# Contiguous transposes for the first two supertiles, and stores that put their rows right

## The chip, the cores and the metric

The kernel runs on one core of a Trainium2 chip. The metric is the device time of one execution in microseconds (us), as the median of several runs. The profile is one execution; its span, from the first to the last instruction, is some 2 us shorter than the device time.

## The reference

A depthwise convolution with a 1x1 window is a scale per channel, and a pointwise convolution is a matrix product over the channels:

```python
# x: (1, 384, 384, 384) bf16, dw: (1, 1, 384), pw: (384, 384)
out = x * dw[0, 0]                            # k = 1, so no padding and one term
return jnp.einsum('bhwc,cd->bhwd', out, pw)
```

So 147456 rows of 384 channels are each multiplied by the same 384x384 matrix, whose rows were scaled by dw. The kernel scales the matrix once, at its start, and not the rows.

## The kernel before

Rows are worked on in *supertiles* of 512, of which there are 288. Supertiles are loaded and stored in *chunks* of L supertiles; chunks make up *groups*, and a group uses one of three input buffers X and one of three output buffers O. The first group has the chunks 1, 1, 2, 2, 4; each group in the middle is one chunk of 10; the last two groups have shrinking chunks.

```python
LMAX, NR = 10, 3
head, tail = [[1, 1, 2, 2, 4]], [[6, 4], [4, 2, 1, 1]]
return head + [[LMAX]] * (mid // LMAX) + tail
# chunks: (g, i, off, first, L): group, place in it, offset in the buffer, first supertile, length
n_parts = [1 if c[0] + 1 < len(groups) else len(PARTS) if c[3] + 1 == NS else 2 for c in chunks]
```

TensorE multiplies over partitions, so the channels must lie on partitions. VectorE does this with transposes of 32x32 blocks of 4-byte words (two channels in a word), two for each supertile (`h` = 0, 1), into one of two buffers T. PSUM has one half of four banks for each of two supertiles. The main loop keeps TensorE on 48 matmuls per supertile, four row tiles side by side:

```python
def supertile(s, rv):
    for b, par in steps:                       # 12 steps
        for q in range(4):                     # PSUM bank q takes the rows from row tile q
            if q == 0 and par == 0 and b in (0, 3):
                nc.tensor.wait_ge(s_t[s][b // 3], rv)          # transposes h = 0, h = 1
            if q == 0 and s == 0:
                for e, v in w_first.get((b, par), []):         # weight casts, early steps
                    nc.tensor.wait_ge(s_wr[e], v)
            mm = nc.tensor.matmul(PS[s][:, q, :D], lhsT=Ts[s][32 * q : 32 * q + 32, b, par::2],
                                  rhs=w_r[32 * q : 32 * q + 32, b, par, :], ...)

# of the scaled matrix, six casts from PSUM: 1 ScalarE, 0 VectorE
w_eng = [1, 0, 1, 1, 1, 1]
# the first step of supertile 0 waits for one cast of VectorE and three of ScalarE
w_first = {(0, 0): [(0, 1), (1, 3)], (4, 0): [(1, 4)], (4, 1): [(1, 5)]}
```

The transposes, in which `k` counts the four rows per partition of a supertile and `i` the 32 partitions of a block:

```python
def transposes(t, j):
    ...
    X, sem, n = x_of(t)
    Xw = X.bitcast(U32).rearrange("p (k l) c -> p k l c", l=L)
    Tw = Ts[s][:].bitcast(U32).rearrange("p b (i k) -> p b k i", k=4)
    for h in range(2):
        if h == 0 and j == 0:
            nc.vector.wait_ge(sem, n)                          # the chunk has landed
        ins = nc.vector.transpose(
            out=Tw[:, 3 * h : 3 * h + 3],
            in_=Xw[:, :, j, 96 * h : 96 * h + 96].rearrange("p k (b w) -> p b k w", w=32),
        )
        if jj >= 2:
            ins._wait_ge(s_pe, 2 * (jj - 2) + h + 1)           # T is free again
        ins.then_inc(s_t[s][h])
```

The innermost run of the output, over `i`, steps 4 words (16 bytes), so that a row's place in T is its place in the supertile. The last supertile has a form of its own (`T<-Xk` in the profile), whose output is one run.

ScalarE copies the four banks of a finished supertile from PSUM to the output buffer O, as bf16:

```python
if j == 0 and i == 0 and g >= NR:                              # the buffer's last stores are out
    nc.scalar.wait_ge(s_o[g % NR], 16 * sum(map(len, groups[g % NR : g : NR])))
a = nc.scalar.copy(Ov[:, :, j, :], PS[s][:, :, :D])            # (p, q, d)
a._wait_ge(s_pe, 2 * jj + 2)
a.then_inc(s_a[s])
```

All loads of the main loop and nearly all stores are issued by SyncE, one after the other, in a fixed order. A group's load waits until the buffer's last supertile has been transposed, and a store until the copy of its last supertile is done:

```python
def store(t, k):
    g, i, off, first, L = chunks[t]
    je = first + L * (k + 1) // n_parts[t] - 1
    src = Os[g % NR][:, 4 * off * D : 4 * (off + L) * D]
    rows = of[512 * first : 512 * (first + L), :]
    if first + 2 < NS:
        dst = rows.rearrange("(q p j) d -> p q (j d)", q=4, p=P)
        src = src.rearrange("p (q e) -> p q e", q=4)
        e = L * D // n_parts[t]
        dst, src = dst[:, :, e * k : e * k + e], src[:, :, e * k : e * k + e]
        nc.sync.wait_ge(s_a[je % 2], je // 2 + 2)
    ...                                                        # the last two supertiles
    eng = nc.scalar if first + 1 == NS and k == 2 else nc.sync
    eng.dma_start(dst, src).then_inc(s_o[g % NR], 16)

for _, f, a in sorted(todo, key=lambda a: a[0]):
    if f is load_x and chunks[a[0]][4] == LMAX and chunks[a[0]][0] == 1:
        nc.sync.wait_ge(x_of(1)[1], 16)
    if f is store and a[0] == 0:
        for _ in range(28):                                    # waits that are over at once: a short delay
            nc.sync.wait_ge(s_pw, 16)
    f(*a)
```

SyncE's order at the start is: the loads of the first group's five chunks, the loads of the second and third group, the stores of chunks 0 to 3, the load of the fourth group, the store of chunk 4, and from there a load and a store of a group in turn.

Of the kernel before, what the change touches and what calls it, by code (L numbers as in the profile page):

```python
# [9 lines left out]
U32 = mybir.dt.uint32  # L10
# [3 lines left out]
NR = 3  # L14
LONG_AT = [8, 148]
PARTS = [slice(0, 4, 2), slice(1, 2), slice(3, 4)]


def _groups(n_super: int):

    head, tail = [[1, 1, 2, 2, 4]], [[6, 4], [4, 2, 1, 1]]
    mid = n_super - sum(map(sum, head + tail))
    assert mid > 0 and mid % LMAX == 0
    return head + [[LMAX]] * (mid // LMAX) + tail
# [3 lines left out]
def kernel(  # L28
# [12 lines left out]
    nc = tc.nc  # L41
# [3 lines left out]
    D = pw.shape[1]  # L45
# [7 lines left out]
    NS = N // 512  # L53
    groups = _groups(NS)

    chunks, first = [], 0
# [2 lines left out]
            chunks.append((g, i, sum(ls[:i]), first, L))  # L59
            first += L  # L60
    NT = len(chunks)
    n_parts = [1 if c[0] + 1 < len(groups) else len(PARTS) if c[3] + 1 == NS else 2 for c in chunks]
    g_end = [max(c[3] + c[4] for c in chunks if c[0] == g) - 1 for g in range(len(groups))]

    consts = ctx.enter_context(tc.tile_pool(name="consts", bufs=1))
# [19 lines left out]
    Ts = [bufp.tile([P, NB, 256], BF16, name=f"T{i}") for i in range(2)]  # L85
# [9 lines left out]
    s_a = [nc.alloc_semaphore(f"s_a{i}") for i in range(2)]  # L95
    s_d = nc.alloc_semaphore("s_d")
    s_o = [nc.alloc_semaphore(f"s_o{i}") for i in range(NR)]
# [10 lines left out]
    with tc.tile_critical(sync_engine=mybir.EngineType.Pool, no_gpsimd_drain=True):  # L108
        def x_of(t):
            g, i, off, first, L = chunks[t]  # L110
            if first + 2 == NS:
                return Xl[:], s_xl, 32
            n = sum(len(ls) > i for ls in groups[g % NR : g + 1 : NR])
            return Xs[g % NR][:, 4 * off : 4 * (off + L), :], s_x[g % NR][i], 16 * n

        def load_x(t, eng=nc.sync):
            g, i, off, first, L = chunks[t]
            dst, sem, _ = x_of(t)
            rows = xf[512 * first : 512 * (first + L), :]
            if first + 2 < NS:  # L120
                src = rows.rearrange("(p s) c -> p (s c)", p=P)
                dst = dst.rearrange("p s c -> p (s c)")
                if i == 0 and g >= NR:
                    je = g_end[g - NR]
                    eng.wait_ge(s_t[je % 2][1], je // 2 + 1)
            else:
                src = rows.rearrange("(a k q) c -> q a k c", k=4, q=4)
            eng.dma_start(dst, src).then_inc(sem, 16)

        def load_last(eng):  # L130
            src = xf[512 * (NS - 1) :, :].rearrange("(m p) c -> p m c", p=P)
            eng.dma_start(Xl[:], src).then_inc(s_xl, 16)

        def store(t, k):
            g, i, off, first, L = chunks[t]
            je = first + L * (k + 1) // n_parts[t] - 1
            src = Os[g % NR][:, 4 * off * D : 4 * (off + L) * D]
            rows = of[512 * first : 512 * (first + L), :]
            if first + 2 < NS:
                dst = rows.rearrange("(q p j) d -> p q (j d)", q=4, p=P)  # L140
                src = src.rearrange("p (q e) -> p q e", q=4)
                e = L * D // n_parts[t]
                dst, src = dst[:, :, e * k : e * k + e], src[:, :, e * k : e * k + e]
                nc.sync.wait_ge(s_a[je % 2], je // 2 + 2)
            elif first + 2 == NS:
                dst = rows.rearrange("(m q) d -> m (q d)", q=4)
                part = slice(2 * D * k, 2 * D * k + 2 * D)
                dst, src = dst[:, part], src[:, part]
                nc.sync.wait_ge(*((s_a[0], NS // 2 + 1) if k == 0 else (s_d, 1)))
            else:  # L150
                dst = rows.rearrange("(m p) d -> p m d", p=P)[:, PARTS[k], :]
                src = src.rearrange("p (m d) -> p m d", d=D)[:, PARTS[k], :]
                if k == 0:
                    nc.sync.wait_ge(s_d, 2)
                    nc.sync.wait_ge(s_a[1], NS // 2 + 1)
                elif k == 1:
                    nc.sync.wait_ge(s_d, 3)
                else:
                    nc.scalar.wait_ge(s_a[1], NS // 2 + 2)
            eng = nc.scalar if first + 1 == NS and k == 2 else nc.sync  # L160
            eng.dma_start(dst, src).then_inc(s_o[g % NR], 16)
# [10 lines left out]
        for t, (g, i, off, first, L) in enumerate(chunks):  # L172
            if 0 < t < NT - 2:
                todo.append((g_end[g - NR] if g >= NR else -1, load_x, (t,)))
            for k in range(n_parts[t] - (first + 1 == NS)):
                todo.append((first + L * (k + 1) // n_parts[t] + 1, store, (t, k)))
        for _, f, a in sorted(todo, key=lambda a: a[0]):
            if f is load_x and chunks[a[0]][4] == LMAX and chunks[a[0]][0] == 1:
                nc.sync.wait_ge(x_of(1)[1], 16)
            if f is store and a[0] == 0:  # L180

                for _ in range(28):
                    nc.sync.wait_ge(s_pw, 16)
            f(*a)
# [128 lines left out]
        for n in range(4):  # L313
            rows = slice(32 * n, 32 * n + 32)
# [3 lines left out]
        for n in range(4):  # L318
            to, h, e = slice(32 * n, 32 * n + 32), n // 2, n % 2
            for g in range(4):  # L320
                rows = slice(32 * g, 32 * g + 32)
# [8 lines left out]
        def transposes(t, j):  # L330
            g, i, off, first, L = chunks[t]
            jj = first + j
            s = jj % 2
            if jj + 1 == NS:
                nc.vector.wait_ge(s_xk, 32)
                Tw = Ts[s][:].bitcast(U32).rearrange("p (v j) (m w) -> p v j m w", v=2, m=4)
                Xw = Xk[:].bitcast(U32).rearrange("p (j v m) w -> p v j m w", v=2, m=4)
                for v in range(2):
                    ins = nc.vector.transpose(out=Tw[:, v], in_=Xw[:, v])  # L339
                    ins._wait_ge(s_pe, 2 * (jj - 2) + v + 1)  # L340
                    ins.then_inc(s_t[s][v])
                return
            X, sem, n = x_of(t)
            Xw = X.bitcast(U32).rearrange("p (k l) c -> p k l c", l=L)
            Tw = Ts[s][:].bitcast(U32).rearrange("p b (i k) -> p b k i", k=4)
            for h in range(2):
                if h == 0 and j == 0:
                    nc.vector.wait_ge(sem, n)
# [4 lines that stand above are left out]
                if jj >= 2:  # L353
                    ins._wait_ge(s_pe, 2 * (jj - 2) + h + 1)
                ins.then_inc(s_t[s][h])

        order = [(t, j) for t in range(NT) for j in range(chunks[t][4])]

# [26 lines left out]
        for jj, (t, j) in enumerate(order):  # L385
            g, i, off, first, L = chunks[t]
            s = jj % 2
            Ov = Os[g % NR][:, 4 * off * D : 4 * (off + L) * D].rearrange("p (q j d) -> p q j d", q=4, d=D)
            if j == 0 and i == 0 and g >= NR:
                nc.scalar.wait_ge(s_o[g % NR], 16 * sum(map(len, groups[g % NR : g : NR])))  # L390
            if jj + 2 == NS:
                nc.vector.wait_ge(s_pe, 2 * jj + 2)
                nc.vector.wait_ge(s_o[g % NR], 16 * sum(map(len, groups[g % NR : g : NR])))
                a = nc.scalar.copy(Ov[:, 0:2, j, :], PS[s][:, 0:2, :D])  # L394
                a._wait_ge(s_pe, 2 * jj + 2)
                a.then_inc(s_a[s])
                nc.vector.tensor_copy(Ov[:, 2:4, j, :], PS[s][:, 2:4, :D]).then_inc(s_d)  # L397
                continue
            if jj + 1 == NS:
                for n, m in enumerate((0, 2, 1, 3)):  # L400
                    o = (nc.scalar.copy if n % 2 else nc.vector.tensor_copy)(Ov[:, m, j, :], PS[s][:, m, :D])  # L401
                    o._wait_ge(s_pe, 2 * jj + 1 + n)
                    o.then_inc(s_a[s] if n % 2 else s_d)
                store(t, 2)
                continue
            a = nc.scalar.copy(Ov[:, :, j, :], PS[s][:, :, :D])  # L406
            a._wait_ge(s_pe, 2 * jj + 2)
            a.then_inc(s_a[s])

            if jj == LONG_AT[0]:  # L410
                load_last(nc.scalar)
            if jj == LONG_AT[1]:
                nc.scalar.wait_ge(s_xk, 32)
                load_x(NT - 2, nc.scalar)
            if jj + 2 < NS:
                transposes(*order[jj + 2])
# [30 lines left out]
```

## Time and profile before

| | |
|---|---|
| device time, median of 3 runs | 574.56 us (574.37 to 574.73) |
| span of the profile | 572.3 us |
| TensorE matmul busy | 567.0 us, 99% |
| VectorE busy | 508.9 us, 89% |
| ScalarE busy | 418.2 us, 73% |
| granted TensorE clock | 1.00 |
| DMA | 226.88 MB, 396 GB/s over the span |

The busy times are sums over the whole span. The chain that ended last follows the work back from the last instruction, at each step to what released it. A group's row gives the busy time, the mean time of one instruction in ns, the idle time of the engine just before the group's instructions, and what ended this idle time. For a DMA, the issue (the time in which SyncE handed it to the queue) and the landing (when its semaphore reached its full count) are different things, and the landing can be much later.

### The profile page before, as it was taken

What the parts mean: (1) busy time and instruction counts of PE and PEld (TensorE: products, weight loads), DVE (VectorE), ACT (ScalarE), POOL (GpSimd) and SP (SyncE); (2) the same over time, 40 slices, a digit from 0 to 9 for tenths busy, and PEclk for the clock granted to TensorE, in tenths of its full rate; (3) what the DMA queues carried; (4) which work ended last, traced back from release to release, by engine and by line L of the source; (5) the groups of instructions that cost most, each with busy time, mean ns of one, the idle gap of its engine ahead of it and who ended that gap; (6) DMA issues with size and microseconds to landing.
All of it is one profiled execution on the core that took longest, in us unless ns stands there. A gap on an engine that the chain in (4) does not pass through costs nothing.

```text
span 572.3 us, 29681 instructions
## 1 busy us (share of the span) xinstructions
PE 567.0 (99%) x13835; PEld 414.0 (72%) x13835; DVE 508.9 (89%) x585; ACT 418.2 (73%) x297; POOL 16.9 (3%) x45
## 2 busy tenths in 40 slices
PE   8999999999999999999999999999999999999997
PEld 5777777777777777777777777777777777777774
DVE  7899999999999999999999999999999999999995
ACT  6777777777777777777777777777777777777775
POOL 4042000000000000000000000000000000000000
PEclk9999999999999999999999999999999999999999
DMA  8999999999999999999999999999999999999677
GB/s 328 446 387 424 420 420 424 437 420 419 424 420 412 395 386 434 399 388 400 414 406 396 410 419 392 403 403 432 398 384 422 417 382 390 420 403 386 252 287 256
DMA packets 26896, 226.88 MB, mean 396 GB/s; under 512 B 1285, under 2 KB 7558, under 8 KB 23046
## 3 DMA queue, kind: packets, MB, share of 16 engines
q1 hardware_dynamic: 25696, 225.91, 97.4%
q10 hardware_dynamic: 1190, 0.89, 0.5%
q14 instruction: 9, 0.07, 0.0%
q8 instruction: 1, 0.02, 0.0%
HBM read 113.54 MB, written 113.25 MB: 396 GB/s over the span
## 4 chain that ended last, share of the span: by engine, by line
PE 98%; DMA 1%; DVE 0%; SPq 0%; issue 0%; ACT 0%; POOLq 0%
PE ps L211 98%; DMA X<-in_x_dram 1%; PE ps L279 0%; DVE T L349 0%; ACT O L401 0%; SPq L168 0%; SPq L167 0%; SPq L442 0%; POOLq L108 0%; POOLq L431 0%
## 5 line engine op out<-in xcount | busy, mean ns | idle before, releaser
L211 PE MATMUL ps<-w_r,T 32*128 32x384 bf16 x13776 | 559.8, 321 | 0.4 <-DVE T L349 0.4
L349 DVE STREAM_TRANSPOSE T<-X 128x384 uint32<-128x384 uint32 x572 | 501.6, 880 | 54.5 <-DMA X<-in_x_dram 2.0
L211 PEld LDWEIGHTS ps<-w_r,T 32*128 32x128 bf16 x13776 | 411.6, 93 | 148.7 <-issue 0.8
L406 ACT CAST O<-ps 128x1536 bf16<-128x1536 f32 x286 | 411.3, 1438 | 147.0 <-PE ps L211 147.0
L326 POOL COPY Xk<-Xl 32x256 bf16<-32x256 bf16 (+1 forms) x32 | 10.1, 340 | 22.5 <-DMA Xl<-in_x_dram 21.6
L316 POOL COPY raw<-w_r 32x768 bf16<-32x768 bf16 x8 | 6.4, 819 | 6.6 <-ACT w_r L362 6.4
L362 ACT CAST w_r<-ps 128x768 bf16<-128x768 f32 x5 | 3.6, 820 | 1.0 <-PE ps L261 1.0
L228 PE MATMUL ps<-const-bfloat16-1.0 32*128 32x384 bf16 x24 | 2.4, 513 | 1.1 <-PEq L431 1.1
L261 PE MATMUL ps<-raw 64*128 64x384 bf16 x16 | 2.6, 475 | 0.1
L261 PEld LDWEIGHTS ps<-raw 64*128 64x128 bf16 x16 | 0.8, 114 | 2.2 <-DMA raw<-in_pw_dram 1.2
L328 ACT ACT_TABLE_LOAD x1 | 1.3, 1283 | 1.5 <-PEq L431 1.5
L279 PE MATMUL ps<-raw,T 64*128 64x384 bf16 (+1 forms) x16 | 2.2, 326 | 0.0
L397 DVE CAST O<-ps 128x768 bf16<-128x768 f32 x1 | 1.0, 958 | 1.4 <-PE ps L211 1.4
L349 DVE STREAM_TRANSPOSE T<-Xl 128x384 uint32<-128x384 uint32 x2 | 1.8, 880 | 0.2
L279 PEld LDWEIGHTS ps<-raw,T 64*128 64x128 bf16 (+1 forms) x16 | 1.0, 96 | 1.2 <-issue 0.6
L228 PEld LDWEIGHTS ps<-const-bfloat16-1.0 32*128 32x128 bf16 x24 | 0.6, 117 | 1.4 <-issue 1.4
L401 ACT CAST O<-ps 128x384 bf16<-128x384 f32 x2 | 1.0, 478 | 0.9 <-PE ps L279 0.9
L367 DVE TENSOR_REDUCE sel<-eye 128x64 f32<-128x128 bf16 x1 | 0.3, 289 | 1.5 <-POOL eye L302 1.5
L339 DVE STREAM_TRANSPOSE T<-Xk 128x384 uint32<-128x384 uint32 x2 | 1.2, 580 | 0.5 <-PE ps L211 0.4
L401 DVE CAST O<-ps 128x384 bf16<-128x384 f32 x2 | 1.1, 558 | 0.3 <-PE ps L279 0.2
L362 DVE CAST w_r<-ps 128x768 bf16<-128x768 f32 x1 | 1.0, 957 | 0.5 <-PE ps L261 0.5
L394 ACT CAST O<-ps 128x768 bf16<-128x768 f32 x1 | 0.8, 798 | 0.5 <-PE ps L211 0.5
(10 smaller groups left out, 2.4 us busy)
## 6 DMA issues: line engine op xcount, KB each, us to landing
X<-in_x_dram SPq DMA_DIRECT2D x26, 3840.0 KB, 21.6
out_dram<-O SPq DMA_DIRECT2D x26, 3840.0 KB, 27.6
X<-in_x_dram SPq DMA_DIRECT2D x3, 1536.0 KB, 17.9
out_dram<-O SPq DMA_DIRECT2D x4, 768.0 KB, 8.8
out_dram<-O SPq DMA_DIRECT2D x2, 1536.0 KB, 13.8
X<-in_x_dram SPq DMA_DIRECT2D x3, 768.0 KB, 7.6
X<-in_x_dram SPq DMA_DIRECT2D x1, 2304.0 KB, 19.6
out_dram<-O SPq DMA_DIRECT2D x1, 2304.0 KB, 11.4
```

The costliest lines, as they stand in the source:

```text
L211: mm = nc.tensor.matmul(PS[s][:, q, :D], lhsT=Ts[s][32 * q : 32 * q + 32, b, par::2], rhs=w_r[32 * q : 32 * q + 32, b, par, :], start=(b, ...
L228: nc.tensor.matmul(PS[0][:, 2 * (i % 2) + i // 2, :D], lhsT=ones[32 * i : 32 * i + 32, 0:P], rhs=ones[32 * i : 32 * i + 32, :], start=True ...
L261: mm = nc.tensor.matmul(PS[(k + 1) % 2][:, 2 * r + v, :D], lhsT=sel_w[64 * v : 64 * v + 64, k, r, :, :].rearrange("p q w -> p (q w)"), rhs ...
L279: return nc.tensor.matmul(PS[1][:, m, :D], lhsT=Tk[rows, at : at + P, par], rhs=w_k[rows, k, par, :], start=start, stop=stop, tile_positio ...
L316: nc.gpsimd.tensor_copy(w_k[rows, k], w_r[rows, b]).then_inc(s_wk)
L326: nc.gpsimd.tensor_copy(dst, src).then_inc(s_xk)
L328: nc.scalar.copy(warm[:, s : s + 1], nc.const_aps.tensor(0.0, [P, 1], F32)).then_inc(s_a[s])
L339: ins = nc.vector.transpose(out=Tw[:, v], in_=Xw[:, v])
L349: ins = nc.vector.transpose(out=Tw[:, 3 * h : 3 * h + 3], in_=Xw[:, :, j, 96 * h : 96 * h + 96].rearrange("p k (b w) -> p b k w", w=32),)
L362: o = nc.vector.tensor_copy(out, in_) if e == 0 else nc.scalar.copy(out, in_)
L401: o = (nc.scalar.copy if n % 2 else nc.vector.tensor_copy)(Ov[:, m, j, :], PS[s][:, m, :D])
L406: a = nc.scalar.copy(Ov[:, :, j, :], PS[s][:, :, :D])
```

## The change

The transposes of supertiles 0 and 1 write T in one run (`k i` in place of `i k`), which is meant to take VectorE less time, at the start, when TensorE waits for the first of them. The rows of T then stand in another order: PSUM bank q, partition p = 32 k + i, now holds row 128 q + 4 i + k of the supertile. The stores of these two supertiles put this right. In the changed code the four stores of such a supertile are the four banks: store number k takes the 128 partitions of bank k and writes them to its 128 rows, in DRAM in the order (k, i) of extents 4 and 32. In place of one store of 512 rows there are so four of 128 rows, each row a run of 768 bytes as before. The counts for which ScalarE and VectorE wait before they write to a used output buffer follow.

```diff
-    n_parts = [1 if c[0] + 1 < len(groups) else len(PARTS) if c[3] + 1 == NS else 2 for c in chunks]
+    n_parts = [(4 if t < 2 else 1) if c[0] + 1 < len(groups) else len(PARTS) if c[3] + 1 == NS else 2 for t, c in enumerate(chunks)]
@@ store
-            if first + 2 < NS:
+            if t < 2:
+                dst, src = rows.rearrange("(q i k) d -> q k i d", q=4, k=4)[k], src[:, D * k : D * k + D]
+                if k == 0:
+                    nc.sync.wait_ge(s_a[first % 2], first // 2 + 2)
+            elif first + 2 < NS:
@@ the delay, now before the first of the four stores alone
-            if f is store and a[0] == 0:
+            if f is store and a == (0, 0):
@@ transposes
-            Tw = Ts[s][:].bitcast(U32).rearrange("p b (i k) -> p b k i", k=4)
+            Tw = Ts[s][:].bitcast(U32).rearrange(
+                "p b (k i) -> p b k i" if t < 2 else "p b (i k) -> p b k i", k=4
+            )
@@ waits for a used output buffer (twice)
+        def o_free(g):
+            return 16 * sum(n_parts[t] for t, c in enumerate(chunks) if c[0] < g and c[0] % NR == g % NR)
-                nc.scalar.wait_ge(s_o[g % NR], 16 * sum(map(len, groups[g % NR : g : NR])))
+                nc.scalar.wait_ge(s_o[g % NR], o_free(g))
```

More of the change, by code (lines that the diff above doesn't have):

```diff
@@ L389 @@
             if j == 0 and i == 0 and g >= NR:
-                nc.scalar.wait_ge(s_o[g % NR], 16 * sum(map(len, groups[g % NR : g : NR])))
+                nc.scalar.wait_ge(s_o[g % NR], o_free(g))
             if jj + 2 == NS:
                 nc.vector.wait_ge(s_pe, 2 * jj + 2)
-                nc.vector.wait_ge(s_o[g % NR], 16 * sum(map(len, groups[g % NR : g : NR])))
+                nc.vector.wait_ge(s_o[g % NR], o_free(g))
                 a = nc.scalar.copy(Ov[:, 0:2, j, :], PS[s][:, 0:2, :D])
```

## The prediction

> **What bounds the kernel now.** I read the busy table and the cost groups of the page, then the chain that ended last in order of time, then the timeline of the first 30 us, then the SyncE queue's issues with their time to landing, at the start and at the end.
>
> The page (engine busy line of the chain, and groups: line, engine, operation, tiles, shapes, count | busy us, mean ns | idle us before, releaser):
>
> ```profile
> PE 98%; DMA 1%; DVE 0%; SPq 0%; issue 0%; ACT 0%; POOLq 0%
> ...
> L211 PE MATMUL ps<-w_r,T 32*128 32x384 bf16 x13776 | 559.8, 321 | 0.4 <-DVE T L349 0.4
> L349 DVE STREAM_TRANSPOSE T<-X 128x384 uint32<-128x384 uint32 x572 | 501.6, 880 | 54.5 <-DMA X<-in_x_dram 2.0
> ...
> L339 DVE STREAM_TRANSPOSE T<-Xk 128x384 uint32<-128x384 uint32 x2 | 1.2, 580 | 0.5 <-PE ps L211 0.4
> ```
>
> TensorE's main loop takes 559.8 us of the 572.3 us span and was kept waiting 0.4 us in all, once, by the first transpose. So the time is set by when this stream starts, by its length, and by what follows its end. The last two rows give the price of the layout: the same 128x384 transpose takes 880 ns where it writes words 16 bytes apart (L349) and 580 ns where it writes one run (L339, last supertile).
>
> The chain that ended last, its start (start us, length us, what):
>
> ```profile
> 1.87 3.76 DMA X<-in_x_dram
> 5.63 0.02 issue
> 5.66 0.88 DVE T L349
> 6.53 0.09 issue
> 6.62 559.83 PE ps L211 x13776
> ```
>
> The first transpose alone stands between the landing of the input and 559.83 us of unbroken TensorE. Timelines of this stretch (start, length, engine, line, operation, count [idle before]); the first block is the window 4.9 to 5.6 us:
>
> ```profile
> 4.12 2.20 ACT L362 CAST w_r<-ps 128x768 bf16<-128x768 f32 x3 [1.00 <-PE ps L261]
> ```
>
> ```profile
> 4.12 3.61 ACT L362 CAST w_r<-ps 128x768 bf16<-128x768 f32 x5 [1.00 <-PE ps L261]
> 5.66 2.96 DVE L349 STREAM_TRANSPOSE T<-X 128x384 uint32<-128x384 uint32 x4 [0.26 <-DMA X<-in_x_dram]
> 9.16 14.18 DVE L349 STREAM_TRANSPOSE T<-X 128x384 uint32<-128x384 uint32 x16 [0.54 <-DMA X<-in_x_dram]
> 24.51 5.64 DVE L349 STREAM_TRANSPOSE T<-X 128x384 uint32<-128x384 uint32 x7 [1.17 <-DMA X<-in_x_dram]
> ```
>
> The first matmul also waits for three weight casts on ScalarE, which end at 4.12 + 2.20 = 6.32 us, hidden now behind the transpose that ends at 6.53.
>
> The store queue, SyncE's L161: the third store (16.1 us), then the stores issued at 476.3, 562.1 and 567.3 us:
>
> ```profile
> L161 SPq DMA_DIRECT2D out_dram<-O x1: 13357/13357/13357, 16.1 to 16.1; - x1
> DMA to landing us min/median/max: 23.3/23.3/23.3
> ...
> L161 SPq DMA_DIRECT2D out_dram<-O x1: 372/372/372, 476.3 to 476.3; - x1
> DMA to landing us min/median/max: 29.2/29.2/29.2
> ...
> DMA to landing us min/median/max: 4.4/4.4/4.4
> ...
> DMA to landing us min/median/max: 1.9/1.9/1.9
> ```
>
> Two things show. The issue of the third store took 13.4 us where others take 0.4: the queue takes no more until transfers ahead of it move on. And a backlog of DMA is carried through the whole kernel and gone only at about 568.6 us, when the last stores are issued. The semaphore records of single DMA engines say whose it is: of the store issued at 476.3 us, 15 engines are done between 493.5 and 496.6 us and one at 505.5. That one engine finishes a load and a store of a long group every 19.55 us, all kernel long, against the 19.5 us that TensorE needs for ten supertiles; it is never idle.
>
> [...] the second load of Xl, whose DRAM side begins with an extent of 4, never has more than 4 packets in flight, and with the first one it shows 21 increments on their semaphore, where two loads on all engines would give 32. [...] the first two stores, issued at 10.3 and 12.2 us, landed at 35.4 and 37.2, behind the loads of 3840 KB that landed at 24.4 and 34.1. [...]
>
> **The change, part by part.**
>
> (1) Four transposes, of supertiles 0 and 1, go from 880 to 580 ns. The first then ends at 5.66 + 0.58 = 6.24 us. The casts, at 6.32, are now later, so TensorE can start at 6.32 + 0.08 (the lead 6.62 - 6.53, rounded) = 6.40 us instead of 6.62: 0.22 us won, not 0.30. The fourth and fifth casts end at about 7.0 and 7.73 us and are needed after 32 and 40 of a supertile's 48 matmuls (1.95 us in all), at 6.40 + 1.30 = 7.70 and 6.40 + 1.63 = 8.03: no new wait. The other three transposes were early already. Supertile 2 waits for its load: transpose from 9.16 to 10.04, needed at 6.40 + 3.90 = 10.30. Supertile 10: 24.51 + 0.88 = 25.39, needed at 6.40 + 19.5 = 25.90. Both hold, so the 0.22 us stays on the path to the end.
>
> (2) Two stores of 512 rows become eight of 128 rows, of the same 768 bytes each. Six more issues of about 0.4 us are 2.4 us of SyncE, which has nothing else to do there. But the new destination is (4, 32, 384), outermost extent 4, so each of the eight runs on 4 engines[...]. A 768-byte packet takes 36 ns in the trace. 1024 packets are 1024 x 36 / 16 = 2.3 us on all engines now and 1024 x 36 / 4 = 9.2 us on four after.
>
> (3) Four engines are thus 6.9 us later than they would be. No engine of the compute path feels that by itself: the load issued at 33.16 us lands at 50.6 now, about 57 after, and is first needed near 63; the stores of the first group, out at 54.4 now, about 61 after, must be out when ScalarE reuses their buffer at 67.
>
> (4) What may be felt is the other twelve. If the queue fills by engine, the eight stores fill the four rings with 264 descriptors (32 rows and an increment, eight times), where two stores of 33 went before the queue stuck. SyncE then gets one small store in per 32 x 36 ns = 1.2 us from about 33 us, and the stores of supertiles 2 to 5 and the next load are issued near 38 to 41 us instead of 29.5, 33.1 and 34.5. From about 34 us the twelve, the slow one among them (the second Xl load, on the four, put hardly any delay on it), have nothing to do for some 4 to 5 us, less the 2.5 us of work that they no longer have: 1.5 to 2.5 us of lag on the one engine that never catches up. At the end its slack is about 0.5 us: it is level at 568.6, has some 2.1 us of stores to come, and the last landing is at 571.2. So the end moves by 1 to 2 us.
>
> Sum: -0.22 us if the queue doesn't hold the twelve up; otherwise about +1 to +2 us, as the end is then set by a DMA engine and the 0.22 us no longer counts.
>
> **The rivals.**
> A. Only the start counts: 574.56 - 0.22 = 574.3 us. For it: PE's 98% of the chain, and 10 us of slack on every load. Against it: the backlog that ends with the kernel.
> B. The slow engine's lag reaches the end: 575.5 to 576.6 us. For it: the 13.4 us issue, the outermost extent of 4, and landing times that fall to 1.9 us only at the last stores. Against it: I can't tell from the trace whether the limit is one ring or the sum of all; with the sum, the twelve get their next stores in time, and even gain 2 us.
> C. The lag of the four grows beyond the 6 us of slack at 57 to 63 us and TensorE waits for a load or ScalarE for a buffer: 577 us and more. Against it: the sum under (3).
> D. The full 0.30 us is won as casts and transposes move together: 574.26 us. Against it: the casts' end at 6.32 depends on nothing that changes.
>
> **Range and chances.** I give A and D together 0.45, B 0.5, C 0.05, and choose a value between the two heaps, 575.0 us, since I can't choose between them; 574.1 is A less the spread of the runs (574.37 to 574.73), 576.9 is B with some more lag. Two per cent would be 11.5 us; nothing here comes near it: 0.003 faster, 0.987 within, 0.01 slower.
>
> **What would show it.** Step 1: four transposes of about 580 ns and TensorE's first L211 at about 6.40 us, released by the cast L362. Step 2: eight small stores with four engine increments each, landing about 1.2 us apart from 35 to 45 us. Step 4: the next load issued near 40 us instead of 33.2, mean DMA share near a half from 34 to 38 us, and the last stores landing well over 2 us after their issue. If those stores land in 2 us, A holds. I am wrong if the transposes still take 880 ns, if the stores run on 16 engines, or if TensorE shows new idle time.

## The result and the profile after

| | before | after |
|---|---|---|
| device time, median | 574.64 us (574.37 to 574.75) | 582.05 us (581.85 to 583.86) |
| span of the profile | 572.3 us | 580.0 us |
| ratio after / before | | 1.0137, 95% interval 1.0116 to 1.0157 |

The change costs 7.4 us. The main groups of the page after (line, engine, operation, tiles, shapes, count | busy us, mean ns | idle us before, releaser):

```profile
L215 PE MATMUL ps<-w_r,T 32*128 32x384 bf16 x13776 | 559.8, 321 | 0.5 <-DVE T L355 0.5
L355 DVE STREAM_TRANSPOSE T<-X 128x384 uint32<-128x384 uint32 x572 | 499.5, 876 | 57.0 <-DMA X<-in_x_dram 3.6
```

TensorE's stream is as it was: 559.8 us of work, 0.5 us of waiting. So the 7.4 us don't lie in it. The chain that ended last (start, length, what) tells the same from its two ends:

```profile
1.87 4.18 DMA X<-in_x_dram
6.05 0.02 issue
6.08 0.59 DVE T L355
6.67 0.09 issue
6.76 559.83 PE ps L215 x13776
566.59 2.18 PE ps L283 x16
568.77 0.02 issue
568.79 0.48 ACT O L410
```

The first transpose is down from 0.88 to 0.59 us. The input landed 0.42 us later in this profile (6.05 against 5.63 us), so TensorE starts at 6.76 us, but only 0.71 us after the landing where it was 0.99. All computing is done at 569.3 us (569.1 before). After it come 10.7 us in which only stores are left. The transposes of the first two supertiles, as a group of the window 5 to 9 us:

```profile
L355 DVE STREAM_TRANSPOSE T<-X 128x384 uint32<-128x384 uint32 x4 | 2.0, 556 | 0.9 <-DMA X<-in_x_dram 0.9
```

Now the other engines of the story, the queue and the DMA. SyncE's issues from 10 to 44 us (start, length, line, count), before:

```profile
10.33 22.78 SPq L161 DMA_DIRECT2D out_dram<-O  x4
33.16 1.39 SPq L128 DMA_DIRECT2D X<-in_x_dram  x1
```

and after, where the ten stores are the eight small ones and those of chunks 2 and 3:

```profile
10.47 28.81 SPq L165 DMA_DIRECT2D out_dram<-O  x10
39.33 1.23 SPq L128 DMA_DIRECT2D X<-in_x_dram  x1
40.60 1.19 SPq L165 DMA_DIRECT2D out_dram<-O  x1
```

The load of the fourth group goes out at 39.33 us in place of 33.16. What the DMA engines do meanwhile, by stretches (the stretch and its length; busy time and, as x, instructions of TensorE, its weight loads, VectorE, ScalarE and GpSimd; the granted clock; last the mean busy share of the 16 DMA engines and GB/s), before:

```profile
34.00:36.00 2.00, 2.00 (x56) 1.48 (x52) 1.81 (x3) 1.44 (x1) 0.01 (x1) 1.00 1.10 381
36.00:38.00 2.00, 2.00 (x57) 1.45 (x49) 1.76 (x3) 1.44 (x1) 1.86 (x6) 1.00 1.07 397
```

and after:

```profile
32.00:34.00 2.00, 2.00 (x56) 1.50 (x52) 1.81 (x3) 1.44 (x1) 0.00 (x0) 1.00 0.62 212
34.00:36.00 2.00, 2.00 (x56) 1.47 (x51) 1.81 (x3) 1.44 (x1) 0.96 (x3) 1.00 0.29 97
36.00:38.00 2.00, 2.00 (x59) 1.50 (x52) 1.81 (x3) 1.44 (x1) 1.82 (x7) 1.00 0.27 93
38.00:40.00 2.00, 2.00 (x56) 1.50 (x52) 1.81 (x3) 1.44 (x1) 1.83 (x7) 1.00 0.73 249
```

A share of 0.27 to 0.29 is four engines of sixteen and little else (from 34 to 38 us the trace has 4.5 packets in flight on average and never under 4, where it had 17.2 before): twelve stand idle while TensorE, beside them, does its full 2.00 us in each stretch. Nothing waits for them at this time. Their delay shows 530 us later. The two loads issued at 511 us, before and after (time to landing):

```profile
L128 SPq DMA_DIRECT2D X<-in_x_dram x2: 335/399/463, 510.9 to 511.2; - x2
...
DMA to landing us min/median/max: 17.9/18.7/19.4
```

```profile
L128 SPq DMA_DIRECT2D X<-in_x_dram x2: 327/390/452, 511.0 to 511.4; - x2
...
DMA to landing us min/median/max: 26.9/27.7/28.4
```

They are issued at the same time and land 9 us later. At the end the queue is stuck again. Seven stores took 7.35 us to issue before, most of it waiting for their copies, and take 11.3 us after (before, then after):

```profile
562.12 7.35 SPq L161 DMA_DIRECT2D out_dram<-O  x7
```

```profile
562.25 11.34 SPq L165 DMA_DIRECT2D out_dram<-O  x7
```

The last of them is issued at 572.87 us in place of 568.99, and lands at 578.9 us in place of 570.9. Of all increments of these last stores only six come after 575.1 us, one by one from 576.0 to 578.9: I take them for those of one engine, which is late while fifteen have nothing left to do.

In what follows, **lag** means this: the trace records 16 increments of a load's semaphore (from 48.30 to 50.58 us for the load issued at 33.16 us in the kernel before), and I take them for one from each of its 16 engines. The lag of a kernel at a load is the time of the last of the 16, less the same in the kernel before. From about 120 us on the last increment comes well after the other fifteen (1.3 us after the next at the load issued at 121 us in the changed kernel, 3.2 in the one before, and more later), and I take it for that of the slow engine (the one that finishes a group in 19.55 us). At the first loads of the changed kernels it can be that of one of the four engines instead.

### The profile page after: what moved, and what is told of

Same layout as the page of the kernel before. It is cut to its first block, busy times and chain, and to the rows that moved or that the text cites. A ratio compares the mean times of both kernels' runs of the same rounds, so it can differ in the third digit from the quotient of the medians.

```text
span 580.0 us, 29687 instructions
## 1 busy us (share of the span) xinstructions
PE 567.0 (98%) x13835; PEld 419.9 (72%) x13835; DVE 506.8 (87%) x585; ACT 418.3 (72%) x297; POOL 16.9 (3%) x45
## 4 chain that ended last, share of the span: by engine, by line
PE 97%; DMA 1%; SPq 0%; DVE 0%; issue 0%; ACT 0%; POOLq 0%
PE ps L215 97%; DMA X<-in_x_dram 1%; PE ps L283 0%; DVE T L355 0%; ACT O L410 0%; SPq L172 0%; SPq L171 0%; SPq L451 0%; POOLq L108 0%; POOLq L440 0%
## 5 line engine op out<-in xcount | busy, mean ns | idle before, releaser
L215 PE MATMUL ps<-w_r,T 32*128 32x384 bf16 x13776 | 559.8, 321 | 0.5 <-DVE T L355 0.5
L215 PEld LDWEIGHTS ps<-w_r,T 32*128 32x128 bf16 x13776 | 417.2, 93 | 143.2 <-issue 1.0
```

## The experiments

My theory after the result was the prediction's rival B, made larger: the eight stores run on four engines, the queue takes no more rows for these four, SyncE sticks (16.8 us at the third store), the twelve other engines run dry, and the slow engine among them never gets the time back. The rivals were a cost in the transposes, six more DMAs, strided rows in DRAM, and the extra packets of the four engines as such.

**Each half alone.** The first kernel has the new transposes and the old stores, so 1024 output rows stand in another order:

```diff
-            Tw = Ts[s][:].bitcast(U32).rearrange("p b (i k) -> p b k i", k=4)
+            Tw = Ts[s][:].bitcast(U32).rearrange(
+                "p b (k i) -> p b k i" if t < 2 else "p b (i k) -> p b k i", k=4)
```

> The contiguous transposes of the first two supertiles with the two stores of the kernel before; those 1024 output rows stand in another order. Theory (the loss is all in the stores; the transposes save 0.2 to 0.3 us at the start): 574.4 us, that is 0.1 to 0.3 us under the kernel before, four transposes of about 580 ns, the last store landing 2 us after its issue. Rival (the transposes themselves cost something later, by another order of T in the matmuls): near 582 us.

Measured: 574.70 us, ratio 0.9999 (0.9991 to 1.0008). TensorE starts 0.71 us after the input's landing here too. So 0.28 us are saved at that place, but the interval of the whole time, half a microsecond to each side, is too wide to show it. No cost of the transposes shows either.

The second is the changed kernel with the old transposes (again those rows in another order):

```diff
-                "p b (k i) -> p b k i" if t < 2 else "p b (i k) -> p b k i", k=4
+                "p b (i k) -> p b k i", k=4
```

> The old transposes of 880 ns with the eight new stores; those 1024 output rows stand in another order. Theory (the stores on four engines hold the queue, the slow engine never catches up): 581.5 to 583 us, the load of the fourth group issued near 39 us. Rival (the loss needs the transposes): near 574.6 us.

Measured: 581.74 us (578.57 to 583.69), ratio 1.0125 (1.0109 to 1.0140). The load of the fourth group left at 39.88 us in the profiled run. The loss is in the stores.

**The same stores on 16 engines.** Eight stores, 128 rows of 768 bytes each, as in the change, but cut the other way: one k over four banks.

```diff
-                dst, src = rows.rearrange("(q i k) d -> q k i d", q=4, k=4)[k], src[:, D * k : D * k + D]
+                dst = rows.rearrange("(q i k) d -> k i q d", q=4, k=4)[k]
+                src = src[32 * k : 32 * k + 32, :].rearrange("p (q d) -> p q d", q=4)
```

> As the changed kernel, with eight stores of 128 rows of 768 bytes too, but each takes the 32 partitions of one k over all four banks, so that both sides begin with an extent of 32 and the store runs on 16 engines. Theory (four engines are the cause): the whole loss goes, 574.3 to 574.6 us, the load of the fourth group issued near 33 us. Rival (six more DMAs on the queue, or the strided rows in DRAM, are the cause): 580 us or more.

Measured: 574.72 us, ratio 0.9999 (0.9991 to 1.0007). SyncE's issues here:

```profile
11.69 21.65 SPq L166 DMA_DIRECT2D out_dram<-O  x10
33.38 1.88 SPq L128 DMA_DIRECT2D X<-in_x_dram  x1
```

Ten stores again, and the load leaves at 33.38 us. Neither the number of DMAs nor the strided rows in DRAM show a cost (the interval is half a microsecond to each side); the outermost extent of 4, with the four engines that it leaves, does (581.74 us with the stores alone). This also answers what the prediction left open: the queue took all eight of these in at once, 1024 rows, and only stuck at the store after them, while of the four-engine stores it stuck at the third, with 256 rows taken. That is 64 rows for each engine in use in both cases (256 on 4 and, as I take it, 1024 on 16), and so it was in the kernel before, where the third store's issue took 13.4 us, with 1024 rows taken. In these runs the limit goes by the rows of one engine, not by the sum of all.

**Idle time alone.** The kernel before, all stores on 16 engines, no work added; SyncE is only held before the store of chunk 2:

```diff
+            if f is store and a[0] == 2:
+                nc.sync.wait_ge(s_a[0], 10)      # copy of supertile 16; below 14: (s_a[0], 9), 15: (s_a[1], 9)
```

> The kernel before, with nothing changed but that SyncE waits for the copy of supertile 16 (about 41.4 us) before it issues the store of chunk 2, so that the store of chunk 2 and all behind it enter the queue some 12 us later and the DMA engines are idle from about 36 us on. All stores on 16 engines, no added work. Theory (idle time of the slow engine early on is never made up and comes out at the end): its first lag is 5 us, and the time is 579 to 584 us, with TensorE as unbroken as before. Rival (the extra work of four engines is what is late, idle time alone is made up in 500 us): 574.6 us.

> The kernel before, with SyncE held until the copy of supertile 14 (about 37.5 us) before the store of chunk 2; no work added, all stores on 16 engines. The slow engine's first lag should be 3 us. Theory with a lag that stays as it is: 574.6 + 3 - 0.5, 577.1 us. Theory with a lag that grows once the slow engine's loads fall together with the others' loads: 578 to 580 us.

> As before, with SyncE held until the copy of supertile 15 (about 39.4 us): a first lag of about 5 us, like that of the changed kernel, with no store on four engines. Theory with a lag that stays: 579.1 us. Theory with a lag that grows as it did in the changed kernel (4.5 to 9 us): 581 to 584 us. Rival (four engines' extra packets are needed for the loss): 574.6 us.

Measured: 585.46 us (583.38 to 588.10) held to supertile 16, 583.65 us (582.88 to 586.10; ratio 1.0169, 1.0142 to 1.0196) to 14, and 583.37 us (582.45 to 584.70) to 15. In the first, the computing was held up besides, late in the profiled run: ScalarE waited for stores to free its output buffers, and TensorE for ScalarE (engine, line, what it waited for: us in total, times, longest):

```profile
ACT O L408 <- DMA out_dram<-O: 3.4, 3, 1.6
PE ps L213 <- ACT O L408: 2.3, 2, 1.5
```

That is the way of rival C, and here it took a lag of about 15 us. In the other two ScalarE waited 0.7 and 1.0 us for a store, and TensorE didn't wait for it.

The kernel held to 14, by stretches (columns as above):

```profile
34.00:36.00 2.00, 2.00 (x56) 1.48 (x52) 1.81 (x3) 1.49 (x2) 0.12 (x1) 1.00 0.78 263
36.00:38.00 2.00, 2.00 (x59) 1.47 (x50) 1.81 (x3) 1.49 (x2) 1.82 (x7) 1.00 0.06 19
38.00:40.00 2.00, 2.00 (x56) 1.50 (x52) 1.81 (x3) 1.49 (x2) 1.82 (x7) 1.00 0.44 159
```

and its two loads at 511 us:

```profile
L128 SPq DMA_DIRECT2D X<-in_x_dram x2: 328/390/453, 511.5 to 511.9; - x2
...
DMA to landing us min/median/max: 28.2/29.0/29.7
```

About three microseconds in which the DMA has next to nothing to do, with no other change, cost 9 us at the end. Four engines' extra packets are not needed for the loss. The sizes were off in all three: the lags began at about 10, 4.3 and 6 us where I had 5, 3 and 5: a transfer's first packet moves only some time after its issue begins (1.0 us for the first load of the kernel before, issued at 0.96 us), and in the profiled runs TensorE, and with it the release, was late itself, most in the first (issue at 43.4 us for 41.4). And they grew.

**The backlog taken away.** The changed kernel, with nine tenths of the fourth group's output not stored (that one store moves 384 KB in place of 3840):

```diff
+                e = D if g == 3 else e
                 dst, src = dst[:, :, e * k : e * k + e], src[:, :, e * k : e * k + e]
```

> The changed kernel, but of the fourth group (supertiles 30 to 39) only one row in ten is stored: 384 KB in place of 3840, so nine tenths of that group's output are left out. TensorE, VectorE and ScalarE do all their work. Theory (the end is set by one DMA engine that is late from 40 us on and never idle, so 9 us less work for it at any time before the end brings the loss back): 574.4 to 575.2 us, the last store landing about 2 us after its issue. Rival (the loss is not a carried backlog): 581 us or more, as the saved transfer lies 470 us before the end.

Measured: 574.44 us, ratio 1.0001 (0.9992 to 1.0010). The lag goes from +4.0 us at the load issued at 82 us to -5.4 at the next, and the whole 7.4 us are gone, though the left-out transfer lies more than 450 us before the end. The loss is a backlog that is carried.

**Half the stores.** The changed kernel with `t < 1` for `t < 2` in its three places: transposes and stores changed for supertile 0 alone, four stores on four engines.

> The changed kernel with transposes and stores changed for supertile 0 alone: four stores on four engines in place of eight. Theory (the queue takes some stores before it sticks; the four are in by about 33 us, when the other twelve engines are still at their last load): no lag of the slow engine, 574.4 to 575.2 us. Rival (each small store costs its share): about half of 7.4 us, 578 us.

Measured: 574.69 us, ratio 1.0002 (0.9992 to 1.0011).

```profile
10.28 25.48 SPq L165 DMA_DIRECT2D out_dram<-O  x7
35.80 1.21 SPq L128 DMA_DIRECT2D X<-in_x_dram  x1
```

The load leaves at 35.80 us. Its last increments, at 52.9 to 53.1 us, are those of the four engines, a lag of 2.5 us; the twelve are done by 50.8 us, 0.3 us after the last increment of before. From 101 us on the lag is 0.3 to 1.2 us. Not half the loss, but none: as I read it, the price isn't set by the number of small stores, but by whether the queue is stuck for longer than the other engines have work.

**Why the lag grows.** It didn't stay as it began. In the changed kernel it is 4.2 to 4.8 us from 101 to 218 us and then climbs to 9.1; held to 14, 5.0 to 5.3 and then 10.9; held to 15, 6.5 to 7.1 and then 10.8. Each time the climb begins as the other engines have made up their own delay (their median is level again at about 240 to 280 us) and the slow one has come to be 14 us and more behind their median. In the kernel before it is 8 to 9 us behind until 472 us, and its loads, of 9.1 us each, lie beside the others' stores; at 14 us and more they lie beside the others' next load, and take 9.1 to 10.3 us. The packets point the same way, but weakly: in the trace of the kernel before (80 to 480 us), a load's packet of 30720 bytes takes 1146 ns on average with no other such packet in flight, and 1246 ns with 8 to 14 others, while the medians are 1140 and 1138 ns. One run was a test by chance: in the profiled run of the stores alone TensorE had started late, so that all loads were issued some 2.2 us later; from 221 us on the slow engine was only 11 to 13 us behind the median, its lag stayed between 4.4 and 5.4 us from 101 us on, and the run took 578.57 us, where the other runs of the same kernel took 581.56 to 583.69. To test it on purpose, all loads were issued three supertiles (5.85 us) later from the sixth group on, in the changed kernel and, as a control, in the one before:

```diff
-                    je = g_end[g - NR]
+                    je = g_end[g - NR] + (3 if g >= 5 else 0)
```

> The changed kernel, but from the sixth group on SyncE issues each load 5.85 us later (when three more supertiles have been transposed), so that fifteen engines run their loads and stores 5.85 us later against the slow one, which has enough queued not to notice. No other work. Theory (the slow engine's lag grows from about 240 us on because its loads have come to fall together with the others' loads, 9.1 us alone against 9.6 to 10.3 us together): behind the median it stays under 12 us, the lag stays near 4.5 to 5 us, and the time is 578.5 to 579.5 us. Rival (the growth is the slow engine's own, or comes with the length of its backlog): 581.5 to 583.5 us as in the changed kernel.

> The same shift of the loads in the kernel before, as a control: 574.4 to 574.9 us under both, as the slow engine is behind the others by 9 us there and would be by 3 to 4. If the shift itself costs time, it shows here.

Measured: 579.87 us (579.13 to 580.19) in the changed kernel and 579.11 us (578.68 to 581.30) in the one before. The control fell: the shift itself makes the slow engine late by 5.2 us, as I read it because its backlog is not yet deep enough in the first groups to bridge it. So the first number says less than I wanted. What can be read are the lags: in the control 4.8 to 5.5 us from 185 us to the end, in the changed kernel 4.6 at 127 us and 6.2 to 6.8 at the end, in both without the climb of 4 to 6 us that the changed kernel and the two held ones have. That fits the explanation, but a clean test was not made: why the lag grows stays open.

**All of them in one table.** Lag of the last load (the last increment at 530.7 us before), and span of the profiled run:

| kernel | lag, us | span, us | span less 572.3 |
|---|---|---|---|
| before | 0 | 572.3 | 0 |
| transposes alone | 0.6 | 572.4 | 0.1 |
| one supertile | 0.4 | 572.2 | -0.1 |
| one store short | -0.8 | 572.1 | -0.2 |
| stores alone | 4.8 | 576.3 | 4.0 |
| loads later, on the one before | 5.2 | 576.5 | 4.2 |
| loads later, on the changed one | 6.2 | 577.4 | 5.1 |
| changed | 9.1 | 580.0 | 7.7 |
| held to 15 | 10.8 | 581.5 | 9.2 |
| held to 14 | 10.9 | 581.6 | 9.3 |
| held to 16 | 15.2 | 585.9 | 13.6 |

The stores on 16 engines stand apart, with 1.4 and 573.6 us: TensorE was late itself in that profile (last section). From a lag of 4.8 us on, the span grows by the lag less 0.8 to 1.6 us; under 1 us of lag it doesn't grow. That is the tail's slack.

## Why the prediction was wrong, step by step

The prediction of 575.0 us, 574.1 to 576.9, was too low by 7 us. Its mechanism was right, in rival B; its sizes were not. Rival C's number, 577 us and more, would have held the result, but only by luck: TensorE never waited for the DMA.

Step (1), right in size, and nothing on the time. The transposes took 535 and 578 ns in turn, and 0.28 us were saved between landing and TensorE's start. Why the transposes with words 16 bytes apart take 880 ns is not shown. In this profile the transpose, ended at 6.67 us, and not the cast released TensorE, as the input landed later.

Step (2), right. Each small store has four packets of 4 bytes at its end, where the other transfers of SyncE have 16 (1248 such packets, 76 times 16 and 8 times 4), and four increments that come as its data lands (and one more, about 0.4 us after its issue ends, at 11.55 us for the first, when none of its data has moved); of the first they come at 34.3 to 34.9 us, and then a store follows each 1.06 us (1.2 predicted), the eighth at 41.7 to 42.3. The 4.5 packets in flight from 34 to 38 us, with several of them queued, I read as all on the same four.

Step (3), right. The next load landed at 57.0 us, for 57 predicted, and neither TensorE nor ScalarE waited for anything because of it.

Step (4), the failing step: "1.5 to 2.5 us of lag on the one engine that never catches up". Two terms were mis-sized. First the lag as it begins. The issues were about where I had them (stores of chunks 2 and 3 at 36.98 and 38.30 us, load at 39.33, for "near 38 to 41 us"), and so was the idle time: the twelve had next to nothing in flight from 34.0 us to the first packet of chunk 2 at 38.8. The store of chunk 2 landed on the twelve at 41.3 to 41.6 us, at most 2.2 us after the 39.4 of before, as predicted. But I took it that the same work takes the same time from there on. The store of chunk 3 landed at 44.3 to 44.9 us, 3.8 us after the 41.1 of before, and the load behind them at 54.0 to 54.8, 4.2 us after the 50.6 of before. The packets of the two stores, of 1536 bytes, took 77.9 ns on average where they took 65.5 before, which makes 0.8 us on the 64 of an engine. Stores on four engines are not needed for it: in the kernel held to 14 these packets took 79.2 ns, and chunk 3 landed 3.1 us after chunk 2 there too (44.9 and 41.8 us), for 1.7 before. Why they are slower after the idle time stays open. Second, I took the lag for constant. It grew to 9.1 us, which I had not thought of at all, and the cause of that is not shown. The term for the end, slack of "about 0.5 us", was near the 0.8 to 1.6 of the table. So the span grew by 7.7 us where the sum had 1 to 2.

The choice of 575.0 us, between two heaps at 574.3 and 576, was a value that neither mechanism would give. Rival A's best argument, 10 us of slack on every load, was true and beside the point: TensorE never waited. The evidence for B was in the profile, in the backlog gone only at the end, and deserved more than half.

## What to carry to other kernels

Here a store whose DRAM pattern began with an extent of 4 ran on four DMA engines (four increments with its data, 582.05 us), and the same rows cut so that both sides began with 32 ran, as I read the 574.72 us, on 16; look at the outermost extent, as the better cut was free here. An issue that stuck, for 16.8 us, held everything behind it in SyncE's queue (the load of the fourth group left at 39.33 us for 33.16), so the price was the idle time of the other engines, and it appeared only past the point where they ran dry. And where DMA runs as long as the computing, look whether the backlog is gone before the last stores: here one engine, as I read its landings 19.5 us apart in the kernel before, was never idle from about 100 us on, and what it had lost at 40 us came out at the end, less about 1 us of slack there, and with what the lag had grown by, though TensorE never waited for a load in between.

## What the runs showed of the hardware

One DMA engine needs 19.55 us for a group's load and store, the others 18.3 us when they run without a pause (in the kernel before, the last increments of the loads landing from 102.6 to 161.2 us are 19.53 to 19.56 us apart, and the medians from 61.9 to 153.4 us 18.3 to 18.4). That this one engine, and not the bandwidth as a whole, sets the end was visible in the increments of single engines (545.6 us for the fifteenth of the store issued at 534.8 us before, 551.6 for the last); the mean DMA share before, 0.69 to 0.87 in five stretches of 3 to 7 us from 545 to 569 us, hides it.

In some profiles (old transposes with new stores, stores on 16 engines, held to 16) TensorE ran its first 3 to 4 us of the main loop with 16 to 28 matmuls in each window of 1 us (those that cross its ends counted) in place of 32 and more, and the loop took 561.4 us in place of 559.83 in the first of these. From its chain:

```profile
7.30 561.41 PE ps L215 x13776
568.71 2.18 PE ps L283 x16
```

The granted clock in the profile reads 1.00 in these stretches, so it has to be seen in the count of matmuls; the cause is not shown. It is one way in which single runs differ by 1 to 2 us, more than the 0.28 us that the new transposes save.
